# Gated linear attention and an MLP on one Trainium2 core: cumulative sums on two array tiles ahead of the scores, chunk 0 in halves of batches, statistics and gain on ScalarE, own buffers for the last chunk

## The chip, the cores and the metric

The kernel runs on one core of a Trainium2 chip. The metric is the device time of one execution in microseconds (us). Three runs of the kernel before took 469.5, 469.87 and 472.64 us; the median is 469.87 us.

## The reference

Four batches, eight heads, 768 positions, head size 48, all in fp32. A gated recurrence runs over the positions; its outputs, with the heads side by side (8 x 48 = 384 columns), are the rows `x` of a layer norm with gain, a two-layer MLP with 1536 hidden columns, and a residual sum:

```python
for t in range(S):
    state = alpha[:, :, t, :, None] * state + np.einsum('bhd,bhe->bhde', k[:, :, t], v[:, :, t])
    y[:, :, t] = np.einsum('bhd,bhde->bhe', q[:, :, t], state)
...
mu = np.mean(x, axis=-1, keepdims=True)
var = np.mean((x - mu) ** 2, axis=-1, keepdims=True)
xn = (x - mu) / np.sqrt(var + 1e-06) * g_ln
ch = np.maximum(xn @ w_ch1, 0.0) @ w_ch2
return (x + ch).astype(np.float32)
```

## The kernel before

**Chunks and batches.** The 768 positions are cut into six chunks `c` of 128, and there are four batches `b`. `attention(c, b)` (line 286) does one chunk of one batch; 24 of these generators exist, with the letters a to x (`a` is chunk 0, batch 0; `e` is chunk 1, batch 0). Chunk 0 is done as one block of 128 positions (`whole`); in the later chunks a block is two halves of 64 positions, which use TensorE as four tiles of 64 x 64.

**One attention.** ScalarE takes the logarithm of alpha into `la` (L299). TensorE sums it along the positions with a triangular matrix into `lps` (L304 for chunk 0, L312 later), and ScalarE makes the factors exp(+) and exp(-) of it (L317, L318). VectorE scales k and q (L320, L322), TensorE transposes them (`tps`, L347), ScalarE copies the transposes out (L352, L354, L357), TensorE makes the scores (`aps`, L364 or L369), VectorE masks them into `at` (L377, L380). TensorE makes the state's update (`ups`, L396), VectorE and GpSimd apply it (L411, L413), ScalarE copies the state into `va` (L403). TensorE makes the output (`yps`, L423), ScalarE copies it to `x` (L427), and `x` goes to DRAM (`kept`, L438) for the residual sum. Then comes the layer norm: VectorE's bn_stats and bn_aggr (L442, L443), ScalarE's Ln and Exp for 1/sqrt(var) (L446, L447), the normalised `xn` (chunk 0: VectorE, L451; later: a product of two columns on VectorE, L454, and ScalarE, L456), three transposes on TensorE (`xps`, L463) and one copy to `xT` on ScalarE (L465). The gain g_ln isn't applied here: it is multiplied into the rounded weights.

**Cumulative sums before.** In chunks 1 to 5 an even batch makes the sums of its own and of the next batch together (L307 to L312). The odd batch's alpha is loaded with its two halves of 64 positions exchanged (`load_exchanged`, line 118: two DMAs), so that the four products (two batches, two halves) lie on the four 64 x 64 tiles.

**Weights.** The MLP's weights come as 64-bit floats. `take_weights(i)` (letters A to L, line 235) loads one of 12 pieces and rounds it to fp32: four or more VectorE instructions (L217, L219, L221, L225, then L228 for w2; for w1 three instructions L232, which also multiply by the gain) and one ScalarE instruction (L223).

**The MLP.** Chunk 0 uses plain products: `hidden(c, j)` (L486) makes hidden columns j of all four batches, 512 columns wide, three products for each of twelve j; `project` (L498) makes the second layer. Chunks 1 to 5 use fast-multiplication schemes with fewer products: `hidden_product` (L733; 15 products in each of two rounds r, with recombination on VectorE, GpSimd and ScalarE, L741 to L776, and ReLUs L785) and `product` (L569; 20 products, L579 to L629). Their combined operands are made by `combine_first` (letter S, L685, on GpSimd: 17 sums over w1, partly in place), `combine_weights` (W, L529, VectorE), `combine_x` (X, L708) and `combine_hidden` (N, L556). The hidden activations of a chunk lie in one buffer `hT` (`bufs=1`), which every chunk uses in turn.

**What sets the order.** Each engine works through its queue in program order. The program order is written out by hand: `ORDER` (line 25) is a string of letters, and each letter lets one generator run to its next `yield`. M is the MLP of all chunks in a row, O loads residual rows, R are the ReLUs. A matmul in fp32 shows as two MATMUL records in the trace, a transpose as one.

Of the kernel before, what the change touches and what calls it, by code (L numbers as in the profile page):

```python
# [25 lines left out]
    "acaaabbadccdbabbaddcccaaaaacbbbaaaabbecccccbbbAadaccfafcbabdbbddefeAAddbafecccgA"  # L26
    "ddddhdbgagdhhCeffbaadhffffebbgaecefjCffiffeBadddfdccbeeccabgggddffccbdAdefffccji"
    "BjhjeeeBCBeDDCDjMMhheBMMkDEEGEeeOMMhMMMMegMMeCGFgGhFFhgGJMMMMihhhhhMMJiJlhhhhfMM"
    "MMEgHHgggegggFHHiiIgOMMMMegiIfeeeKggiKIILLKhlSSSSkkeLMMMWeeWWlgffhhhiikjMMkiiiii"
    "SSSSSfMhhMMOOhhhSgggjhjSSjMlWllffgijgMWfggXWXXmMXXXMMXXiOSMMMMMWOOiiSSijXiXXjjjj"  # L30
    "MMMMMMjkkSSnnkkiMMMMMMWMMjMjMMMMMjjkkMMMMRRjjjiiiRlkMMMkWMMmlnnkkkMMMllMMknkOMMR"
    "RMMMMMMMMllllmmMMMlmlMMMMMRMllllkkmRRRoMRMnjjikMMinnnnRiWWWMNMNNNjMMMnMnNNNmMMNN"
    "NlMppMMojkllkkMkkWMMMjjMRNNlNMMMMMmoooikMMMMMNNNkkMMllMMpMMlMMollmMMXnXnXmmXMXXX"
    "nnnXXMMMMnnMMmFmMmLXMMMMXpMMmmpqMMMMpprrnmMmmmKqpprprMMmnrrMMMMppppMMnpMqMMMMmmo"
    "ooMMMoMMMMOMMMMMpppMMMnnMOOOqJomRRRRMRRoooooMMRMroooMRMMMMMRMMRopqqmmCMpMMmotMNp"
    "ppNNnnRMoonMMNNNqqMMMnmnRMMMMMMMqmNNNNrNooMMqqqqqqNpMMMMopMpsrrMMNNMMqMMoMMoqsqq"
    "NNMsMMMMtttOMMprrqqssMsMppoXXXXXXDXXsssMXsXMMssrttXOOOrMMrMMMMrMMMrMtrrrtttMvMMM"
    "rrMMMMMMtssssuMMMMMMsssMtMMMMrrutttuuuqMMMMMMvRvqtvvMMMMMMRRMMuRRMMMMMRRqqquERMM"
    "vMvMMMttttvxsvRRrsMMsMMMMMMuRNNuuNMMMMMNNqRrNtuuuuMMrMMMuLuNqNNrqMMMMMtNNNNtrvvv"
    "vvvMMwMNvsssMMMMsttttsNwMOOxxMxuMMMNsxMMMtMMsMtuXXvvwwwuwXXXXXXMXwuMMMMMMMMMxxxv"  # L40
    "MMXXMMOMuuuMMMMMMMMMMMMMwxxvwMMMwMMvvMMuwwwwwMMMuMMMMMMMwwMMMMIMMMxxxRxxxRRRRMxM"
    "MMMRRRMMMMMRMORwwxxNNwwRMNNJMMMvvxNMMxNNuNuMMMMMMNNRMMMNMMMMMMMNNMGMMwwxwwMMxxxM"
    "NNMMMMMMNxxwvwMMvvXXMXXXXXOMMMMMMMXXMMMXMMMMMXMMMMMMMRMMMMMMMRRRMRMMMMMRMMAMMMMM"
    "MMKMMMMMMMROOOMMRMMMMMMMMMHRMMMMMRRNNNMMNMMMNNNNMMMMNRMMMMMNNMMMMNMMMNNNMMMMMMMM"
    "NBMMMMMM"
# [4 lines left out]
def kernel(  # L50
# [36 lines left out]
    nc = tc.nc  # L87
# [30 lines left out]
    def load_exchanged(to, src):  # L118

        for h in range(2):  # L120
            nc.sync.dma_start(to[halves[h]].rearrange("t i p d -> t (i p d)"),
                              src[halves[1 - h]].rearrange("t h d -> t (h d)"))

    def load(c, m, names):
# [3 lines left out]
        for n, src in (("a", alpha), ("k", k), ("q", q)):  # L128
            if n in names:
                t = raw.tile([P, 2, 2, NP, D], FP32, name=f"r{n}", tag=f"r{n}")  # L130
                step = 1 if n == "a" else 2
                for i in range(0, 2, step):
                    if n == "a" and c > 0 and i:
                        load_exchanged(t[:, 1], src[bs.start + 1, rows])
                        break
                    nc.sync.dma_start(
                        t[:, i:i + step].rearrange("t b i p d -> t b (i p d)"),
                        src[bs.start + i:bs.start + i + step, rows].rearrange("b t h d -> t b (h d)"))
                raws.update({(n, c, b): t[:, b - bs.start] for b in bs})
# [21 lines left out]
    def load_one(n):  # L161

        c, b = divmod(n, B)
        for n, src in (("a", alpha), ("k", k), ("q", q)):
# [4 lines left out]
            if n == "a" and b % 2:  # L169
                load_exchanged(t, rows)  # L170
            else:
                nc.sync.dma_start(t.rearrange("t i p d -> t (i p d)"),
                                  rows.rearrange("t h d -> t (h d)"))
# [8 lines left out]
    w1 = cpool.tile([P, NF, DF], FP32, name="w1")  # L182
    w2 = cpool.tile([P, NJ, DM], FP32, name="w2")
    small = cpool.tile([P, 2 * NF + 2], FP32, name="small")
    g_col, eps, least, g20 = small[:, :NF], small[:, NF:NF + 1], small[:, NF + 1:NF + 2], small[:, NF + 2:]
# [6 lines left out]
    for i in range(NJ // 2):  # L192
        cs, js = slice(2 * i * P, 2 * (i + 1) * P), slice(2 * i, 2 * (i + 1))
        pieces.append((w1[:, :, cs], w1_src[:, :, cs]))
# [12 lines left out]
    def round_weights(i):  # L207
# [19 lines left out]
        if i >= NJ // 2:  # L227
            stt(out=dst, in0=dst, scalar=2.0 ** -20, in1=hi.bitcast(FP32), op0=AOP.mult,  # L228
                op1=AOP.mult)
            return  # L230
        for f in range(NF):
            stt(out=dst[:, f], in0=dst[:, f], scalar=g20[:, f:f + 1], in1=hi[:, f].bitcast(FP32),  # L232
                op0=AOP.mult, op1=AOP.mult)
# [46 lines left out]
    nc.gpsimd.tensor_scalar_mul(g20, g_col, 2.0 ** -20)  # L280

    x_of, xT_of, hT_of, las, lpss = ({} for _ in range(5))
# [3 lines left out]
    def attention(c, b):  # L286
# [14 lines left out]
        yield  # L301
        if whole:
            lps = ps.tile([P, 512], FP32, name="lps", tag="a", bufs=3)
            nc.tensor.matmul(lps[:, :DM], tri, las.pop((c, b)), start=True, stop=True)  # L304
        elif b % 2 == 0:

            for d in range(2):  # L307
                to = lpss[c, b + d] = ps.tile([P, 512], FP32, name="lps", tag="a", bufs=3)
                a = las.pop((c, b + d))
                for s in range(2):  # L310
                    h = halves[s ^ d]
                    nc.tensor.matmul(to[halves[s], :DM], tri[h, h], a[h], start=True, stop=True)  # L312
        yield
        if not whole:
            lps = lpss.pop((c, b))
# [111 lines left out]
        nc.scalar.copy(out=x, in_=yps.rearrange("t a b d -> t (a b d)"))  # L427
# [12 lines left out]
        stats = work.tile([P, 6], FP32, name="stats", tag="stats")  # L440
        mv = work.tile([P, 2], FP32, name="mv", tag="mv")
        nc.vector.bn_stats(stats, x)  # L442
        nc.vector.bn_aggr(mv, stats)  # L443
        yield
        rstd = work.tile([P, 2], FP32, name="rstd", tag="rstd")
        nc.scalar.activation(out=rstd[:, :1], in_=mv[:, 1:2], func=AFT.Ln, bias=eps)  # L446
        nc.scalar.activation(out=rstd[:, :1], in_=rstd[:, :1], func=AFT.Exp, scale=-0.5)  # L447
        yield
        xn = work.tile([P, DM], FP32, name="xn", tag="xn", bufs=2)
        if whole:  # L450
            nc.vector.tensor_scalar(out=xn, in0=x, scalar1=mv[:, 0:1], scalar2=rstd[:, :1],  # L451
                                    op0=AOP.subtract, op1=AOP.mult)
        else:
            nc.vector.scalar_tensor_tensor(out=rstd[:, 1:], in0=mv[:, 0:1], scalar=-1.0,  # L454
                                           in1=rstd[:, :1], op0=AOP.mult, op1=AOP.mult)
            nc.scalar.activation(out=xn, in_=x, func=AFT.Identity, scale=rstd[:, :1],  # L456
                                 bias=rstd[:, 1:])
# [7 lines left out]
        nc.scalar.copy(out=xT_of[c][:, :, b], in_=xps)  # L465
# [15 lines left out]
    def hidden(c, j):  # L481
        if j == 0:
            hT_of[c] = work.tile([P, NJ, B, P], FP32, name="hT", tag="hT", bufs=1)
        hps = ps.tile([P, B, P], FP32, name="hps", tag="m", bufs=3)
# [357 lines left out]
```

## Time and profile before

| | |
|---|---|
| median of 3 runs | 469.87 us (469.5 to 472.64) |
| the profiled execution itself | 469.91 us |
| its span in the profile | 468.1 us, so 1.8 us lie around the span |
| TensorE (PE) busy | 445.0 us |
| VectorE (DVE) busy | 357.8 us |
| ScalarE (ACT) busy | 214.4 us |
| GpSimd (POOL) busy | 175.4 us |
| mean granted TensorE clock | 0.995 |

In the profile's rows a group is named by line, engine, operation and tile ("L312 PE MATMUL lps<-la,consts"). PEld is TensorE's loading of weights, SPq the queue of DMA issues on SyncE. A time in the timeline counts from the start of the span; the bracket at a row's end is the engine's idle time ahead of it, with what ended it. A matmul's recorded duration overlaps with that of the next one, so the rate of TensorE is read from the distance between starts.

### The profile page before, as it was taken

To read this page: it belongs to the slowest core of one execution; us is meant where nothing else is said; L and a number is where in the kernel's file an instruction comes from. 1 tells how busy PE (TensorE), PEld (TensorE's weight loads), DVE (VectorE), ACT (ScalarE), POOL (GpSimd) and SP (SyncE) were. 2 spreads that over 40 slices of the span, in tenths; PEclk is the share of its full clock that TensorE was granted. 3 is DMA by queue.
4 is the path that set the end of the run, shared out by engine and by line. 5 is a ranking of instruction groups with operands and counts; after the bars stand their busy time and mean duration, and the time that the engine had idled before them with its cause. 6 is when DMAs were issued, how large, how long until landed. Compare 5 with 4: busy or idle time off the path is not lost.

```text
span 468.1 us, 10317 instructions
## 1 busy us (share of the span) xinstructions
PE 445.0 (95%) x4050; PEld 369.2 (79%) x4050; DVE 357.8 (76%) x704; ACT 214.4 (46%) x467; POOL 175.4 (37%) x201
## 2 busy tenths in 40 slices
PE   5978999999999999999999999999999999898996
PEld 4856445656678898988889988899998899887896
DVE  3798998998697888785687685867875787765683
ACT  5377474553435555334664444666333451413200
POOL 1010001167576620436440526550326531444513
PEclk9998999999999999999999999999999999999999
DMA  8978967514312340334530226230132000220001
GB/s 274 253 211 225 279 200 200 159 42 142 115 43 61 77 129 18 87 86 101 139 103 1 68 71 170 88 84 3 56 114 38 1 1 0 95 75 1 1 17 52
DMA packets 58232, 45.42 MB, mean 97 GB/s; under 512 B 26908, under 2 KB 54300, under 8 KB 58184
## 3 DMA queue, kind: packets, MB, share of 16 engines
q1 hardware_dynamic: 57640, 44.63, 34.1%
q8 instruction: 32, 0.52, 0.5%
q10 hardware_dynamic: 544, 0.13, 0.2%
q14 instruction: 16, 0.13, 0.1%
HBM read 35.22 MB, written 9.53 MB: 96 GB/s over the span
## 4 chain that ended last, share of the span: by engine, by line
PE 62%; DVE 22%; POOL 6%; ACT 4%; issue 3%; DMA 2%; SPq 0%; POOLq 0%; DVEq 0%; ACTq 0%
PE ops L569 23%; PE hps L733 20%; PE aps L369 4%; PE hps L486 3%; PE yps L423 3%; PE tps L347 2%; DVE at L380 2%; PE ups L396 2%; DMA ws<-in_moe_w_ch_dram 2%; PE ops L498 2%; DVE ws L225 2%; DVE w L219 1%; DVE ws L529 1%; PE xps L463 1%; DVE sum L556 1%
## 5 line engine op out<-in xcount | busy, mean ns | idle before, releaser
L585 POOL TENSOR_TENSOR ob<-ob,u 128x192 f32<-128x192 f32 x40 | 27.8, 704 | 100.0 <-DVE ob L582 76.0
L733 PE MATMUL hps<-sum,w 128*128 128x256 f32 x240 | 60.8, 385 | 1.9 <-DVE hT L776 1.1
L413 POOL TENSOR_TENSOR st<-st,gate 112x192 f32<-112x192 f32 x36 | 20.7, 576 | 86.8 <-DVE st L411 62.4
L733 PEld LDWEIGHTS hps<-sum,w 128*128 128x128 f32 x240 | 44.1, 190 | 9.4 <-DVE hT L776 1.8
L569 PE MATMUL ops<-w,hT 128*128 128x192 f32 x280 | 50.4, 329 | 0.0
L785 ACT ACTIVATE hT<-hT 128x512 f32<-128x512 f32 x60 | 35.0, 622 | 26.1 <-POOL hT L755 14.3
L569 PEld LDWEIGHTS ops<-w,hT 128*128 128x128 f32 x280 | 45.6, 190 | 1.4 <-DVE sum L556 0.6
L403 ACT COPY va<-st 64x192 f32<-64x192 f32 x80 | 27.8, 347 | 25.1 <-POOL st L413 24.3
L486 PE MATMUL hps<-xT,w 128*128 128x512 f32 x72 | 32.3, 598 | 0.8 <-ACT hT L489 0.8
L498 PE MATMUL ops<-w,hT 128*128 128x384 f32 x96 | 32.4, 489 | 0.0
L733 PE MATMUL hps<-xT,w 128*128 128x256 f32 x120 | 31.5, 385 | 0.8 <-DVE hT L765 0.7
L380 DVE COPY_PREDICATED at<-consts,aps 64x512 f32<-64x512 int32 x40 | 29.2, 731 | 3.3 <-PE aps L369 2.3
L569 PE MATMUL ops<-ws,sum 128*128 128x192 f32 x160 | 29.3, 329 | 0.8 <-DVE u L579 0.8
L569 PE MATMUL ops<-ws,hT 128*128 128x192 f32 x160 | 29.6, 328 | 0.1
L357 ACT COPY at<-tps 64x512 f32<-64x512 f32 (+1 forms) x40 | 23.2, 579 | 11.6 <-PE tps L347 6.9
L369 PEld LDWEIGHTS aps<-at,kT 48*64 48x64 f32 x640 | 22.0, 138 | 8.1 <-issue 5.0
L752 POOL TENSOR_TENSOR hT<-hT,u 128x512 f32<-128x512 f32 x10 | 12.8, 1285 | 40.8 <-DVE u L751 40.7
L579 DVE TENSOR_TENSOR ob<-ops,ob 128x192 f32<-128x192 f32 x50 | 17.5, 352 | 13.5 <-POOL ob L585 4.2
L347 PE MATMUL tps<-consts,qk 128*112 128x128 f32 x176 | 25.7, 278 | 2.2 <-DVE qk L322 1.2
L423 PEld LDWEIGHTS yps<-va,at 128*64 128x64 f32 (+1 forms) x768 | 24.1, 137 | 4.4 <-issue 2.8
L498 PEld LDWEIGHTS ops<-w,hT 128*128 128x128 f32 x96 | 17.7, 190 | 12.2 <-DVE w L228 1.0
L569 PEld LDWEIGHTS ops<-ws,sum 128*128 128x128 f32 x160 | 26.0, 190 | 1.4 <-DVE u L579 1.0
(155 smaller groups left out, 1021.1 us busy)
## 6 DMA issues: line engine op xcount, KB each, us to landing
ws<-in_moe_w_ch_dram SPq DMA_DIRECT2D x12, 768.0 KB, 4.8
kept<-x SPq DMA_DIRECT2D x24, 192.0 KB, 2.4
ob<-kept SPq DMA_DIRECT2D x24, 192.0 KB, 2.9
va<-in_v_dram SPq DMA_DIRECT2D x40, 96.0 KB, 3.4
out_dram<-ob SPq DMA_DIRECT2D x19, 192.0 KB, 1.9
ra<-in_alpha_dram SPq DMA_DIRECT2D x14, 192.0 KB, 4.1
rk<-in_k_dram SPq DMA_DIRECT2D x6, 384.0 KB, 4.0
rq<-in_q_dram SPq DMA_DIRECT2D x6, 384.0 KB, 4.3
```

The source lines that it names most:

```text
L347: nc.tensor.transpose(tps[:, p], qk_of(c, b)[:, i, p].rearrange("p a b -> p (a b)")[:, :R], ident)
L357: nc.scalar.copy(out=at[rows[j], :, j], in_=tv[rows[j]])
L369: nc.tensor.matmul(aps[i][halves[1 - i], p, s], kT[rs, p, s], at[rs, p, i, s], start=True, stop=True)
L380: nc.vector.copy_predicated(out=at[h, :, i], data=aps[i][h], mask=mask[h, h].unsqueeze(1).unsqueeze(1).broadcast_to([HS, NP, 2, HS]))
L403: nc.scalar.copy(out=to[h, s, i], in_=st[h])
L423: nc.tensor.matmul(yps[halves[s], i, p], at[rs, p, i, s], va[rs, 0 if whole else s, i, p], start=True, stop=True)
L486: nc.tensor.matmul(hps, w1[:, f, j * P:(j + 1) * P], xT_of[c][:, f], start=(f == 0), stop=(f == NF - 1))
L498: nc.tensor.matmul(ops_of[b], hT_of[c][:, j, b], w2[:, j], start=(j == 0), stop=(j == NJ - 1))
L569: nc.tensor.matmul(acc, lhs[:, j], rhs[:, j], start=(j == 0), stop=(j == NT - 1))
L585: getattr(nc.gpsimd, f"tensor_{op}")(x, x, y)
L733: nc.tensor.matmul(acc[:, i], w, b, start=True, stop=True)
L785: nc.scalar.activation(out=x, in_=x, func=AFT.Relu)
```

## The change

Seven things change together:

1. **Cumulative sums.** Each batch makes its own sums, on the two tiles (0,0) and (1,1) of the array (each half of the positions to the same half of the output). No alpha is loaded exchanged any more, and an alpha load is one DMA for two batches (in chunk 0 still one for each). In the new program 16 of the 20 sums of chunks 1 to 5 stand directly ahead of another batch's scores `aps`, which use the tiles (0,1) and (1,0); the other four, all of chunk 1, stand in the first part of the program, ahead of `yps`, `ups`, chunk-0 `aps` and `tps`.
2. **Chunk 0 in halves.** `hidden(h, j)` makes the columns of two batches (256 wide instead of 512), so there are 72 products instead of 36, each half as wide; letters Y, Z are the two halves of the first layer, P, Q those of the second. In TensorE's order the first `hps` of chunk 0 now stands after only two of the four `xps` of chunk 0.
3. **Statistics on ScalarE.** The copy to `x` also gives the row sum, a Square with the negative mean as bias gives the row's squared deviations; bn_stats, bn_aggr and the product of two columns leave VectorE.
4. **The gain on ScalarE.** The copy of `xps` to `xT` becomes three ScalarE multiplications by a column of g. The rounding of w1 then ends with one VectorE instruction over 768 columns instead of three over 256.
5. **combine_first on VectorE.** The 17 sums over w1 leave GpSimd, and w1 is laid out by piece.
6. **The last chunk in own buffers.** The hidden activations of chunk 5 lie in `at`, `qk` and `va` buffers, which attention no longer needs then; its sums of x and its scratch lie in other such buffers. The first-layer products of chunk 5 have a letter of their own (V), and `ORDER` mixes them with the second-layer products of chunk 4.
7. **ORDER** is written anew throughout.

The core of the diff:

```diff
-        elif b % 2 == 0:
-            for d in range(2):
-                to = lpss[c, b + d] = ps.tile([P, 512], FP32, name="lps", tag="a", bufs=3)
-                a = las.pop((c, b + d))
-                for s in range(2):
-                    h = halves[s ^ d]
-                    nc.tensor.matmul(to[halves[s], :DM], tri[h, h], a[h], start=True, stop=True)
+        else:
+            for h in halves:
+                nc.tensor.matmul(lps[h, :DM], tri[h, h], a[h], start=True, stop=True)
...
-        nc.scalar.copy(out=x, in_=yps.rearrange("t a b d -> t (a b d)"))
+        act(out=x, in_=yps.rearrange("t a b d -> t (a b d)"), func=AFT.Copy, accum_out=mean)
...
-        nc.vector.bn_stats(stats, x)
-        nc.vector.bn_aggr(mv, stats)
+        nc.scalar.mul(mean, mean, -1.0 / DM)
+        act(out=xn, in_=x, func=AFT.Square, bias=mean, accum_out=dev)
...
-            nc.vector.scalar_tensor_tensor(out=rstd[:, 1:], in0=mv[:, 0:1], scalar=-1.0,
-                                           in1=rstd[:, :1], op0=AOP.mult, op1=AOP.mult)
+            nc.scalar.mul(off, mean, rstd)
...
-        nc.scalar.copy(out=xT_of[c][:, :, b], in_=xps)
+        for f in range(NF):
+            nc.scalar.mul(xT_of[c][:, f, b], xps[:, f], g_col[:, f:f + 1])
...
-        for f in range(NF):
-            stt(out=dst[:, f], in0=dst[:, f], scalar=g20[:, f:f + 1], in1=hi[:, f].bitcast(FP32),
-                op0=AOP.mult, op1=AOP.mult)
+        stt(out=dst, in0=dst, scalar=2.0 ** -20, in1=hi.bitcast(FP32), op0=AOP.mult, op1=AOP.mult)
...
-    def hidden(c, j):
-        hps = ps.tile([P, B, P], FP32, name="hps", tag="m", bufs=3)
+    def hidden(h, j):
+        bs = slice(2 * h, 2 * h + 2)
+        hps = ps.tile([P, 2, P], FP32, name="hps", tag="m", bufs=3)
         for f in range(NF):
-            nc.tensor.matmul(hps, w1[:, f, j * P:(j + 1) * P], xT_of[c][:, f],
+            nc.tensor.matmul(hps, w1[:, j // 2, f, j % 2 * P:][:, :P], xT_of[0][:, f, bs],
...
-        add, sub = nc.gpsimd.tensor_add, nc.gpsimd.tensor_sub
+        add, sub = nc.vector.tensor_add, nc.vector.tensor_sub
...
+    def third_of(c, t, h):
+        if c + 1 == NCB:
+            return late_of["h"][t * 2 + h]
+        return hT_of[c][:, t * NT:(t + 1) * NT, h * HB:(h + 1) * HB]
...
+    def buffers_of_last():
+        va = [raw.tile([P, 2, 2, 2, NP, D], FP32, name="va", tag="va").rearrange(
+            "t b s i p d -> t (b s i p d)") for _ in range(2)]
+        h = [t.rearrange("k p i s t -> k (p i s t)") for t in ats]
+        h += [t.rearrange("t n p i c -> t (n p i c)") for t in qks[:3]]
+        h.append(va[0][:, :NT * HB * P])
...
     def mlp():
+        for c in range(1, NCB):
+            if c + 1 < NCB:
+                yield from hidden_products(c)
             for n in SECOND:
                 yield from product(c, n)
...
-    turns |= {"M": mlp(), "S": combine_first(), "W": combine_weights(), "R": relus(),
+    turns |= {"M": mlp(), "V": hidden_products(NCB - 1), "S": combine_first(), "W": combine_weights(), "R": relus(),
```

## The prediction

> **What bounds the kernel now.** I read the windows by stage first, then TensorE's timeline inside each stage, then the groups for prices. The rows of the windows give start and end, length, then busy time and instructions of PE, PEld, DVE, ACT, POOL, and last granted clock, DMA share and GB/s. The cuts lie at the first `hps` of chunk 0 (46.87), the end of its first layer (80.9), the start of chunk 1's MLP (125.9), the start of chunk 5's MLP (407.4), its second layer (437.5) and the last matmul (464.3).
>
> ```profile
> 0.00:46.87 46.87, 36.29 (x530) 28.66 (x530) 34.52 (x72) 28.56 (x66) 5.17 (x11) 0.96 0.84 241
> 46.87:80.90 34.03, 33.21 (x179) 16.00 (x178) 32.01 (x53) 19.18 (x34) 2.27 (x4) 1.00 0.75 224
> 80.90:125.90 45.00, 43.31 (x330) 27.21 (x331) 39.34 (x72) 21.75 (x47) 22.84 (x29) 1.00 0.38 113
> 125.90:407.40 281.50, 278.71 (x2738) 249.17 (x2737) 214.19 (x436) 133.34 (x299) 120.57 (x133) 1.00 0.26 69
> 407.40:437.50 30.10, 26.89 (x121) 22.42 (x120) 19.12 (x34) 8.63 (x15) 15.81 (x14) 1.00 0.13 39
> 437.50:464.30 26.80, 26.56 (x161) 25.76 (x160) 18.25 (x41) 2.95 (x7) 7.82 (x11) 1.00 0.05 16
> 464.30:468.10 3.80, 0.02 (x1) 0.00 (x0) 0.36 (x1) 0.00 (x0) 0.90 (x2) 0.84 0.30 104
> ```
>
> From 46.87 on TensorE has hardly any gaps; VectorE, the next, has 94% in the second row, 87% in the third, 76% in the fourth. So after 46.87 the time is the length of TensorE's queue, and ahead of it TensorE idles 10.6 us while it waits for others. The other hole is in chunk 5's first layer, which has only itself to run:
>
> ```profile
> 49.99 10.47 PE L486 MATMUL hps<-xT,w 128*128 128x512 f32 x24
> 60.39 1.14 PE L423 MATMUL yps<-va,at 128*64 128x48 f32 x32
> ...
> 177.03 0.88 PE L312 MATMUL lps<-la,consts 64*64 64x384 f32 x8
> 177.84 1.57 PE L569 MATMUL ops<-more,sum 128*128 128x192 f32 x8
> ...
> 409.74 1.13 PE L733 MATMUL hps<-sum,ra 128*128 128x256 f32 x4 [1.36 <-DVE sum L708]
> 410.71 1.03 PE L733 MATMUL hps<-sum,w 128*128 128x256 f32 x4
> 411.57 1.03 PE L733 MATMUL hps<-xT,rk 128*128 128x256 f32 x4
> ...
> 425.60 1.13 PE L733 MATMUL hps<-sum,w 128*128 128x256 f32 x4 [1.10 <-DVE hT L776]
> ```
>
> Prices by distance of starts: 24 matmuls of 512 columns in 60.39 - 49.99 = 10.40 us, 0.433 each; four of 256 columns in 0.86 us, 0.215 each; the cumulative sums of two batches 177.84 - 177.03 = 0.81 us.
>
> A rule to weigh here: the Trainium skill, "Perfetto Trace Analysis", Identifying the Most-Contended Engine, says that matmul busy time misleads and that headroom is judged by MFU and the weight loads' busy share. The page has PEld at 79%, which by that rule would leave 0.21 x 468 = 98 us in TensorE's queue, and a matmul removed would then buy nothing where something else paces. The starts decide: the matmuls of 256 columns follow each other at 0.215 us while one load takes 0.190, so loads are 88% busy in a stretch that has no gap at all. I take the queue as the bound, with about 3 us of stalls in 46.87 to 407.
>
> **The change, part by part.** *Cumulative sums.* Before: ten pairs at 0.81 = 8.1 us. Each batch alone uses two tiles, two passes each, still 0.81 us (the passes of a tile follow each other): 20 x 0.81 = 16.2 us if nothing runs beside. In the program's order 16 of the 20 stand directly ahead of scores on the other two tiles, and TensorE does run ahead on a free tile past an instruction that waits for its own:
>
> ```profile
> 363.08 1.02 PE L369 MATMUL aps<-at,kT 48*64 48x64 f32 x27
> 363.89 0.25 PE L396 MATMUL ups<-rv,qk 64*64 64x48 f32 x1
> 363.95 0.22 PE L369 MATMUL aps<-at,kT 48*64 48x64 f32 x2
> 363.99 0.22 PE L396 MATMUL ups<-rv,qk 64*64 64x48 f32 x1
> ```
>
> All `aps` stand ahead of all `ups` in the program, yet they alternate here. Scores take about 0.95 us (363.08 to the last at 364.06), more than 0.81, so 16 sums should vanish under them. Left are the four early ones, 3.2 us. That is -4.9 us, and five pairs that stood between full-array products no longer break that mode: I give this another -0.7 us, between 0 and -1.0 (0.2 us at most for each). A rule speaks against it: the Trainium skill, "TensorEngine Tiling (Array Packing)", Gotcha 1: PSUM Pressure, says that different row tiles cannot access one PSUM bank at the same time, and both halves of a batch's `lps` now lie in one tile of 512 columns. By the rule a sum takes 1.6 us, 0.65 us sticks out of the scores, and 16 x 0.65 + 4 x 1.6 = 17 us replaces 8.1: +9 us. But the pairs of before also put two row tiles into each `lps`, and the four still took 0.81 us. I take the row.
>
> *Halves in chunk 0.* 144 matmuls at 0.215 = 31.0 us against 72 at 0.433 = 31.2: nothing, on the path. Each needs `xT` of two batches. Ahead of the first `hps` TensorE's queue now lacks a batch's `tps` (0.44 us), one `aps` with `ups` (1.44), one `yps` (1.07) and two `xps` (0.66), and has 0.8 more of sums: 2.8 us of work moves behind it. VectorE's queue there loses four batches' bn_stats and aggregates (4 x 0.73 us), two `xn` (1.0), and parts of roundings and masks that ORDER puts later; by program order and the rows' means it holds some 9 us less. So the first `hps` could come 0 to 9 us sooner; I take 6, as ACT and the loads (DMA 84% of the stretch) do not get shorter. Gain: 6 - 2.8 = 3.2 us, rounded to -3, between +3 and -6.
>
> *Statistics and gain.* VectorE loses per run 13.2 (L442) + 4.4 (L443) + 5.4 (L454) + 0.6 (L682), and 7.7 - 5.8 = 1.9 at the roundings (L232 against six of 0.96, L228's undisturbed price): 25.5 us. It hardly waits on the path after 80 us, so this is worth nothing there by itself; its use is room for combine_first. ScalarE gains: 24 small products at 0.20 (L447) 4.9; 24 Squares, whose price lies between 0.49 (L318, no column) and 0.71 (L456, two columns), 0.65 with its sum, 15.6; 20 products of columns at 0.29 (L446) 5.8; 72 scaled copies of 128 columns at 0.40 (L446 plus 127 columns at 0.85 ns, from L427 and L741) 28.8, less the 11.4 of L465; the row sum in L427, 0 to 0.2 each, 2.4; halved ReLUs +2. Together +48, to 262 us or 57% of the span. In the first 126 us, where eight batches fall, it is +17 on 69.5: 69% of the stretch. That is cover enough on average; behind each late ACT instruction stand the copies of `tps` and the ReLUs that free the `hps` banks, for which PE waits. I charge +2 us for new waits, between 0 and +8.
>
> *combine_first.* 15 sums of 512 columns at 0.69 (L556) and four of 256 at 0.46: 12.2 us more on VectorE against 26.8 less on GpSimd (L685). It overwrites w1 in place, so its later sums wait until chunk 0's last `hps` has read w1, and what VectorE holds behind them waits too; but by program order VectorE is then some 10 us ahead of TensorE. W's sums, 1.48 us where both engines work on SBUF and 0.94 elsewhere, get shorter by up to 4 us. Net on the path 0.
>
> *Loads.* Four alpha loads of two batches lose two DMA issues each (1.2 us of SPq for the two), six single ones lose one. The order of the rest stays; hidden behind SP's other issues: 0 to -1, inside the early term.
>
> *Last chunk.* 120 matmuls at 0.215 = 25.9 us took 437.53 - 407.36 = 30.2: 4.3 us of stalls, in the timeline as waits for L708, L765, L776, where VectorE and GpSimd trail. Mixed with chunk 4's second layer (160 matmuls) each has other work to stand on: -4, between 0 and -4.5. The end stays: 3.8 us after the last matmul.
>
> **Sum.** -4.9 - 0.7 + 0 - 3 + 2 - 4 = -10.6 us. From the profiled execution, 469.9 us (468.1 of span and 1.8 around it; the median of the runs is the same 469.87), this gives 459.3, so 459 us.
>
> **The rivals.** *A, the early gain or the last chunk's fails:* the first `hps` comes no sooner, since loads hold it (3 + 2.8 us back: 465), or GpSimd's chain at the end still sets the pace (4 back: 463), or both (469); mid 466. For it: DMA at 84%. Against: DVE's 34.5 us of 46.87 with the statistics in the middle of it. *B, the sums do not hide:* either the order between tiles or the bank rule holds; 16 x 0.81 = 13 us come back: 472 us, no change. For it: no row shows sums and scores together. Against: the alternating rows above. *C, slower: ScalarE becomes what TensorE waits for.* Each attention adds 48 / 24 = 2.0 us of serial ScalarE work; if 0.6 us of each turns into a PE wait, 24 x 0.6 = 14 us cancel the gain plus the margin, and a full 1.2 us gives 459 + 29 - 2 = 486. For it: the statistics, the gain, copies and ReLUs all queue on one engine in the first 126 us. Against: at 69% there, and of PE's waits on ACT the profile has under 5 us in all. *D, the change doesn't shorten TensorE's queue* is B.
>
> **How the numbers follow.** The likeliest case, all steps within their bounds: 0.69, own range 452 to 465, prediction 459. A: 0.13. B: 0.07. C: 0.11. The range leaves out about 0.07 below 452 (the stalls of the middle vanish as well) and 0.12 above 470: 452 to 470. A per cent, 4.7 us, is about what a measurement of this kernel can tell from no change. Faster by over 1% (under 465.2): the first case and a third of A, 0.73. Within 1%: the rest of A and most of B, 0.15. Slower (over 474.6): C and a little of B, 0.12.
>
> **What would show it.** `lps` rows whose starts lie among `aps` rows with no gap behind them: right; the full-array product after them 1.7 us or more after the first `lps`: B. First `hps` of chunk 0 at about 41 us: right; at 46 or later: A. Chunk 5's first-layer products without bracketed waits over 0.5 us: right. VectorE's busy time about 345 us, ScalarE's about 262, GpSimd's about 147. If PE's waits for ACT sum to over 10 us, C; the prediction is wrong above all if TensorE's gaps after the first `hps` grow.

## The result, and the profile after

The changed kernel takes 458.52 us (median of four runs, 458.32 to 459.46); the kernel before took 470.29 us (median of four, 469.5 to 472.64) beside it. The ratio is 0.9746 with a 95% interval of 0.9707 to 0.9784: faster by 2.5%. The prediction was 459.0. The profiled execution took 459.46 us with a span of 457.7 us, 1.8 us around it as before.

The busy times of the changed kernel, from its page, and then its windows, cut at the first `hps` of chunk 0 (38.23), inside the stage up to chunk 1's MLP, at the start of chunk 5's MLP (380.15) and at 420.1. The columns are those of the windows before: start and end, length, PE, PEld, DVE, ACT, POOL, granted clock, DMA share, GB/s.

```profile
PE 441.1 (96%) x4122; PEld 381.0 (83%) x4122; DVE 338.5 (74%) x626; ACT 249.8 (55%) x643; POOL 152.3 (33%) x164
```

```profile
0.00:38.23 38.23, 31.46 (x417) 23.96 (x418) 27.24 (x57) 25.19 (x63) 4.30 (x9) 1.00 0.86 259
38.23:60.00 21.77, 21.00 (x304) 17.54 (x302) 18.32 (x29) 19.59 (x52) 2.57 (x5) 1.00 0.86 256
...
80.00:100.00 20.00, 18.81 (x171) 14.60 (x170) 17.56 (x28) 14.78 (x40) 4.17 (x4) 1.00 0.63 189
100.00:127.00 27.00, 25.89 (x214) 16.46 (x213) 24.89 (x39) 11.00 (x26) 2.52 (x2) 1.00 0.28 75
127.00:380.00 253.00, 250.90 (x2356) 223.46 (x2354) 186.24 (x352) 149.32 (x390) 103.83 (x108) 1.00 0.27 73
380.00:420.10 40.10, 40.05 (x206) 36.19 (x206) 30.39 (x60) 8.24 (x16) 19.48 (x17) 1.00 0.07 21
```

Three things are to be seen. Ahead of the first `hps` TensorE idles 38.23 - 31.46 = 6.8 us, where it idled 10.6 before. In the stretch from 380 to 420, where most of chunk 5's first layer now lies, it idles 0.05 us; in the stretch of that layer in the kernel before it idled 3.2. And from 38 to 127 TensorE still has small holes (3.9 us in 88.8, the row not shown among them), with ScalarE at 90% in the second row and VectorE at 92% in the fourth.

The sums and the scores, in TensorE's timeline (start, duration, then line, tile and shape; the `ups` in the last row is the next step):

```profile
65.03 0.54 PE L289 MATMUL lps<-la,consts 64*64 64x384 f32 x2
65.20 0.40 PE L344 MATMUL aps<-at,kT 48*64 48x64 f32 x6
65.40 0.49 PE L289 MATMUL lps<-la,consts 64*64 64x384 f32 x2
65.42 0.80 PE L344 MATMUL aps<-at,kT 48*64 48x64 f32 x21
66.01 0.25 PE L371 MATMUL ups<-rv,more 64*64 64x48 f32 x1
```

The 32 scores begin 0.17 us after the sums and run between and beside their four passes; sums and scores together take 66.01 - 65.03 = 0.98 us. Scores alone took 0.81 up to the next `ups` in the kernel before, sums alone 0.81.

**Where the time came from.** In either trace I add up the distances from each matmul's start to the next one's, by line. From the first matmul's start to the last one's it is 461.2 us before and 450.8 after, 10.4 less. The MLP products of chunks 1 to 5 (`hps` and `ops`) account for 274.8 before and 265.6 after: -9.1. Sums and scores of chunks 1 to 5 account for 29.2 and 27.1: -2.1. All the rest, the early stage above all, comes out 0.8 longer. Of the 9.1 us, 4.0 are the stalls of chunk 5's first layer (4.25 beyond 0.216 us for each product before, 0.26 after). The other 5.1 lie in the middle (125.9 to 407.3 us before, 138.6 to 380 after): 76 places before, 44 after, at which the step from a full-array product to the next matmul lasted 0.02 to 0.3 us longer than the usual 0.216 (`hps`) or 0.163 us (`ops`), mostly by 0.09 or 0.10 (7.7 against 4.7 us in sum), and the longer stalls there (2.7 against 0.7 us).

The granted clock differs too. In the windows of the kernel before, cut at the clock's own steps, TensorE is busy 1.50 of 3.41 us, and in the next 3.42 us it runs at half clock:

```profile
36.78:40.19 3.41, 1.50 (x24) 0.89 (x16) 3.30 (x8) 3.33 (x9) 0.00 (x0) 1.00 1.10 322
40.19:43.61 3.42, 3.39 (x39) 3.30 (x40) 2.47 (x6) 2.44 (x8) 1.05 (x2) 0.50 0.88 210
```

3.4 us at half clock cost up to 1.7 us. The changed kernel has no such step before its last matmul.

### The profile page after: what moved, and what is told of

The parts are those of the page before. It is cut to its first block, busy times and chain, and to the rows that moved or that the text cites. A ratio compares the mean times of both kernels' runs of the same rounds, so it can differ in the third digit from the quotient of the medians.

```text
span 457.7 us, 10476 instructions
## 1 busy us (share of the span) xinstructions
PE 441.1 (96%) x4122; PEld 381.0 (83%) x4122; DVE 338.5 (74%) x626; ACT 249.8 (55%) x643; POOL 152.3 (33%) x164
## 4 chain that ended last, share of the span: by engine, by line
PE 64%; DVE 14%; ACT 10%; POOL 5%; DMA 3%; issue 3%; POOLq 0%; SPq 0%; DVEq 0%; ACTq 0%
PE ops L573 24%; PE hps L750 23%; PE ops L474 4%; DMA gate<-row 3%; PE tps L322 3%; PE aps L344 2%; PE yps L398 2%; POOL ob L589 2%; DVE ws L213 2%; DVE w L207 2%; PE ups L371 1%; PE xps L436 1%; DVE w L215 1%; DVE sum L724 1%; ACT at L332 1%
## 5 line engine op out<-in xcount | busy, mean ns | idle before, releaser
L750 PE MATMUL hps<-sum,w 128*128 128x256 f32 x192 | 47.8, 381 | 0.1
L750 PEld LDWEIGHTS hps<-sum,w 128*128 128x128 f32 x192 | 35.4, 190 | 5.7 <-ACT hT L758 0.9
L573 PE MATMUL ops<-w,hT 128*128 128x192 f32 x224 | 39.8, 327 | 0.0
L573 PEld LDWEIGHTS ops<-w,hT 128*128 128x128 f32 x224 | 36.5, 190 | 0.7 <-DVE ob L583 0.2
L462 PE MATMUL hps<-xT,w 128*128 128x256 f32 x144 | 34.2, 383 | 0.5 <-ACT hT L465 0.5
L583 DVE TENSOR_TENSOR ob<-ops,ob 128x192 f32<-128x192 f32 x50 | 17.4, 352 | 20.6 <-POOL ob L589 10.8
L750 PE MATMUL hps<-xT,w 128*128 128x256 f32 x120 | 31.2, 383 | 0.2 <-DVE hT L782 0.2
L439 ACT ACTIVATE xT<-xps,small 128x128 f32<-128x128 f32 x72 | 20.9, 366 | 18.7 <-PE xps L436 18.6
L462 PEld LDWEIGHTS hps<-xT,w 128*128 128x128 f32 x144 | 26.1, 190 | 4.3 <-ACT hT L465 0.9
L801 ACT ACTIVATE hT<-hT 128x512 f32<-128x512 f32 x48 | 27.6, 623 | 3.4 <-DVE hT L782 1.6
L474 PEld LDWEIGHTS ops<-w,hT 128*128 128x128 f32 x96 | 17.8, 190 | 12.6 <-DVE w L215 1.4
L398 PE MATMUL yps<-va,at 128*64 128x48 f32 (+1 forms) x768 | 26.9, 224 | 1.4 <-ACT xT L439 0.7
L322 PEld LDWEIGHTS tps<-consts,qk 128*112 128x112 f32 x176 | 19.3, 134 | 7.2 <-ACT at L332 1.9
```

The lines of the kernel that those rows point to most:

```text
L322: nc.tensor.transpose(tps[:, p], qk_of(c, b)[:, i, p].rearrange("p a b -> p (a b)")[:, :R], ident)
L398: nc.tensor.matmul(yps[halves[s], i, p], at[rs, p, i, s], va[rs, 0 if whole else s, i, p], start=True, stop=True)
L439: nc.scalar.mul(xT_of[c][:, f, b], xps[:, f], g_col[:, f:f + 1])
L462: nc.tensor.matmul(hps, w1[:, j // 2, f, j % 2 * P:][:, :P], xT_of[0][:, f, bs], start=(f == 0), stop=(f == NF - 1))
L474: nc.tensor.matmul(ops_of[b], hT_of[c][:, j, b], w2[:, j], start=(j == 0), stop=(j == NJ - 1))
L573: nc.tensor.matmul(acc, lhs[:, j], rhs[:, j], start=(j == 0), stop=(j == NT - 1))
```

## The experiments

The theory after reading the two traces: the gain is the sums under the scores, the mixed last chunk and fewer breaks, and the moves between VectorE, ScalarE and GpSimd are worth nothing by themselves. The rival: these moves, with the order laid out for them, are what carries the gain. "More than the changed kernel" is the distance between medians, to 458.52 us, taken on another chip (the kernel before has medians of 469.83 to 470.43 us on the five chips used, so 0.6 us can't be told from nothing); a distance to the kernel before is taken from its runs on the same chip.

**Sums on the whole array.** One product with a block-diagonal 128 x 128 triangle takes the place of the two on two tiles:

```diff
-            for h in halves:
-                nc.tensor.matmul(lps[h, :DM], tri[h, h], a[h], start=True, stop=True)
+            nc.tensor.matmul(lps[:, :DM], both, a, start=True, stop=True)
```

> The changed kernel (458.5 us) with the cumulative sums of chunks 1 to 5 made by one product with a block-diagonal triangle on the whole array, in the same places. Such a product costs 2 x 0.323 = 0.65 us and can't run beside the scores. If the sums vanish under the scores and TensorE's queue is the bound, 16 of them come out of their cover and break the full-array mode, 16 x (0.65 + 0 to 0.2), and the four early ones change by -0.16 each: +10 to +13 us, 468 to 472 us. If the sums were not hidden in the changed kernel, or were not on the path: within 2 us of 458.5.

Measured: 464.48 us (ratio 0.9879, 0.9835 to 0.9923), 6.0 more than the changed kernel: about half of what hiding was to be worth. Its timeline at the same place of the program as above:

```profile
63.94 0.81 PE L289 MATMUL lps<-la,consts 128*128 128x384 f32 x2
64.68 1.02 PE L344 MATMUL aps<-at,kT 48*64 48x64 f32 x27
65.49 0.25 PE L371 MATMUL ups<-rv,more 64*64 64x48 f32 x1
```

Nothing overlaps now: 0.74 for the sum, 0.81 for the scores, 1.55 against 0.98. So the hiding is shown. In the later chunks a pair took 0.91 to 0.94 up to `ups`, so a hidden sum stuck out 0.10 to 0.13 there, and nothing where a full-array product follows (1.15 against 1.13). What was off is where it counts: chunk 1's MLP began at 138.26 us here and at 138.61 in the changed kernel. Six of the sixteen hidden sums lie ahead of that point. From the first `hps` (37.22 here, 38.23 there) to it, this kernel takes 101.05 us against 100.39: six uncovered sums, 3.4 us at 0.57 each, cost 0.7, so the early stage isn't set by the length of TensorE's queue. The ten behind it make the loss: 5.0 us between the two traces from there to the last matmul, where ten at 0.63 would be 6.3.

**Own sums alone, in the old order.** In the kernel before, each batch makes its own sums at its own place, without the exchanged loads:

```diff
-        if whole:
-            lps = ps.tile([P, 512], FP32, name="lps", tag="a", bufs=3)
...
+        lps = ps.tile([P, 512], FP32, name="lps", tag="a", bufs=3)
+        a = las.pop((c, b))
...
+            for h in halves:
+                nc.tensor.matmul(lps[h, :DM], tri[h, h], a[h], start=True, stop=True)
```

> The kernel before (470.3 us) with each batch making its own sums on two tiles and no exchanged load, but in the old order, in which they don't stand ahead of scores. If the gain lies in the place beside the scores: 20 x 0.81 instead of 10 x 0.81, +8 us, and up to 2 us more for mode changes, so 477 to 480 us. If the gain lay in the simpler loads and the shorter wait for a partner batch: 466 to 470 us.

Measured: 479.01 us (ratio 1.0187, 1.0137 to 1.0236), as expected: 8.8 us slower than the kernel before. The sums are a gain only at the places that the new order gives them. Here the half clock lasted 6.8 us instead of 3.4, which is part of it.

**The last chunk in turn.** The end of ORDER is rewritten, so that chunk 4's second layer ends before chunk 5's first begins; the buffers stay as changed:

```diff
-    "XXXMMVVRNXXXXMMMXNXMVVVNVVVVVVXNMMMNVVXMNMMVVVRVVVVVVMNMVVVVVVVVAMMMNVVNRRMMMRRR"
...
+    "XXXMMRNXXXXMMMXNXMNXNMMMNXMNMMMNMAMMMNNMMMMMNNMMNOMMMMMMMOMMMOOLVVVVVVVVVVVVVVVV"
...
```

> The changed kernel with the rest of chunk 4's second layer first and chunk 5's first layer after it, in turn, own buffers kept. If the mixing is what removed the stalls of chunk 5's first layer: +4 us, 462 to 463 us, with waits of TensorE for VectorE's results between the products. If the own buffers or a lighter VectorE did it: 458 to 459.5 us.

Measured: 462.08 us (ratio 0.983, 0.9787 to 0.9873), as expected: the mixing is worth 3.6 us. The own buffers weren't undone by themselves.

**Statistics back on VectorE.** bn_stats, bn_aggr and the product of two columns return to VectorE, at the steps where they stood:

```diff
-        nc.scalar.mul(mean, mean, -1.0 / DM)
-        act(out=xn, in_=x, func=AFT.Square, bias=mean, accum_out=dev)
+        nc.vector.bn_stats(stats, x)
+        nc.vector.bn_aggr(mv, stats)
...
-            nc.scalar.mul(off, mean, rstd)
+            nc.vector.scalar_tensor_tensor(out=off, in0=mv[:, 0:1], scalar=-1.0, in1=rstd,
+                                           op0=AOP.mult, op1=AOP.mult)
```

> The changed kernel with bn_stats, bn_aggr and the product of two columns back on VectorE (+23 us of VectorE, -25 of ScalarE). If TensorE's queue is the bound and the early gain comes from the order of chunk 0: 457.5 to 460.5 us, the first product of chunk 0 within 2 us of 38.2. If the early gain comes from a VectorE freed of the statistics: that product 3 to 6 us later, 462 to 465 us.

Measured: 484.12 us (ratio 1.0321, 1.0255 to 1.0387), 25.6 more than the changed kernel. Both expectations missed, and by the largest step of the study. Chunk 1's MLP began at 137.46, even 1.15 us earlier; all of the loss came later. One place, in the timelines of ScalarE, VectorE and TensorE of this kernel in turn (the bracket is the idle time ahead, and what ended it):

```profile
338.28 0.29 ACT L424 ACTIVATE few<-mv,small 128x1 f32<-128x1 f32 x1 [6.63 <-DVE mv L422]
...
341.44 1.16 ACT L332 COPY at<-tps 64x512 f32<-64x512 f32 x2
342.62 0.59 ACT L327 COPY kT<-tps 112x512 f32<-112x512 f32 x1
...
346.83 1.30 ACT L433 ACTIVATE xn<-x,few 128x384 f32<-128x384 f32 x2 [3.02 <-DVE few L431]
```

```profile
344.44 1.46 DVE L355 COPY_PREDICATED at<-consts,aps 64x512 f32<-64x512 int32 x2 [2.02 <-PE aps L344]
...
346.65 0.21 DVE L431 SCALAR_TENSOR_TENSOR few<-mv,few 128x1 f32<-128x1 f32 x2
```

```profile
343.26 1.02 PE L344 MATMUL aps<-at,kT 48*64 48x64 f32 x27 [1.51 <-ACT kT L327]
...
348.19 0.90 PE L439 MATMUL xps<-consts,xn 128*128 128x128 f32 x3 [3.43 <-ACT xn L433]
348.88 2.77 PE L576 MATMUL ops<-ws,sum 128*128 128x192 f32 x8
```

Read it from the top. ScalarE stands 6.63 us at Ln, for which VectorE's `mv` is late. Behind Ln in its queue are the copies of the transposes, so `kT` is late, and TensorE waits 1.51 us for its scores. VectorE waits 2.02 us for these scores with its mask, and behind the mask in its queue stands the product of two columns, for which ScalarE waits with `xn` 3.02 us, and TensorE with `xps` 3.43 us. The last row is the price on top: eight products take 2.77 us where they take 1.46 otherwise, at half clock (347.08 to 353.9); TensorE had stood still for 2.32 of the 3.41 us from 343.67 to 347.08. In this trace half clock lasts 13.7 us before the last matmul, in the changed kernel none.

**VectorE's load without the chain.** The changed kernel, with bn_stats and bn_aggr issued as well, for nobody:

```diff
         act(out=xn, in_=x, func=AFT.Square, bias=mean, accum_out=dev)
+        nc.vector.bn_stats(stats, x)
+        nc.vector.bn_aggr(mv, stats)
```

> The changed kernel, with bn_stats and bn_aggr of x issued on VectorE as well, at the place where the kernel before had them, and their results read by nobody: VectorE gets 24 x 0.73 = 17.5 us of work back and waits for x as before, but the chain x, Square, Ln, Exp, xn stays on ScalarE. Theory H (what cost e3_stats_on_vector its 25.6 us is the chain's two handovers between ScalarE and VectorE, inside the distance that the order leaves between x and xps): 458 to 463 us. Rival L (VectorE's load itself is what TensorE ends up waiting for, through late roundings, masks and sums): 470 us or more, most of the 25.6.

Measured: 463.69 us (ratio 0.9866, 0.9847 to 0.9886), 5.2 more than the changed kernel, and just past the upper end of what theory H gave it. The load alone is some 5 of the 25.6 us; it comes little by little (chunk 2's MLP is 1.9 us later, chunk 3's 3.3, chunk 4's 4.5). The other 20 are not VectorE's load: they come with the handovers and with the half clock that goes with these waits (13.7 us of it, which cost up to 6.9), and these two weren't measured apart. Nor is the early stage bound by the amount of VectorE's work: 6.6 us of these instructions stand ahead of chunk 1's MLP, which begins only 0.75 us later (139.36).

**Statistics on VectorE, but earlier.** bn_stats, bn_aggr and the negated mean stand two steps of the order earlier, and Ln, Exp, the product of two columns and `xn` are all on ScalarE:

```diff
             carry(0, raws["v", c + 1, b][1])
+        nc.vector.bn_stats(stats, x)
+        nc.vector.bn_aggr(mv, stats)
+        nc.vector.tensor_scalar_mul(mean, mv[:, 0:1], -1.0)
```

> The changed kernel with bn_stats and bn_aggr on VectorE as in e3_stats_on_vector, but issued two steps of the order earlier (with the carry of the state, when x has long been copied), with the mean negated there too, so that from Ln to xn the chain runs on ScalarE alone: VectorE has some 22 us more than in the changed kernel and ScalarE some 29 us less, but neither engine waits for the other between x and xps. Theory H (the handovers inside the short distance cost e3_stats_on_vector its 25.6 us, and VectorE's load costs the 5.2 us of e8_stats_beside): 461 to 466 us. Rival (statistics on VectorE are dear in this order wherever they stand): 470 us or more.

Measured: 469.29 us over ten runs (466.5 to 470.97; ratio 0.9987, 0.9963 to 1.001), 10.8 more than the changed kernel: outside both expectations. Taking away one handover and giving the other more room returns 15 of the 25.6 us. The remaining one is still there in the waits of this kernel (engine, tile and line; the releaser; us in total, times, longest):

```profile
ACT few L425 <- DVE mv L417: 18.9, 9, 5.3
```

In the kernel with both handovers the like wait was 36.5 us in 14 places, and a second one, for the product of columns, 26.5 us in 16. Half clock lasted 10.2 us in this trace. The two of the ten runs at a mean clock of 1.0 took 466.5 and 467.06 us, so the half clock is about 2.5 us of the median. With 5.2 for the load some 3 us are left for the remaining handover; this division is worked out, not measured apart.

**Statistics on ScalarE alone, in the old order.** The same move as in the change, made in the kernel before:

```diff
-        nc.scalar.copy(out=x, in_=yps.rearrange("t a b d -> t (a b d)"))
+        act(out=x, in_=yps.rearrange("t a b d -> t (a b d)"), func=AFT.Copy, accum_out=mean)
...
-        nc.vector.bn_stats(stats, x)
-        nc.vector.bn_aggr(mv, stats)
...
+        act(out=xn, in_=x, func=AFT.Square, bias=mean, accum_out=dev)
```

> The kernel before, in its old order, with only the statistics moved to ScalarE (row sum in the copy to x, Square with its sum, no bn_stats, no bn_aggr); the gain stays in the weights. Theory (worth nothing on the path by itself, as the prediction's step said; the order of before leaves room for the chain on either engine): 468 to 472 us. Rival 1 (VectorE's 17.5 us less is a gain of its own in any order): 460 to 466. Rival 2 (ScalarE's 17 us more in the first 126 us delays TensorE): 474 or more.

Measured: 473.47 us (ratio 1.0068, 1.0046 to 1.009), between the theory and rival 2: 3.6 us slower than the kernel before on that chip (469.83). The first `hps` came at 50.72 instead of 46.87, and chunks 1 to 5 begin 2.2 to 4.3 us later than there; half clock lasted 6.8 us instead of 3.4. So the move is a small loss in the old order, and it is what the new order needs.

**Statistics split by chunk.** VectorE for chunks 0 and 1, ScalarE for the rest:

```diff
+        early = c < 2
...
-            nc.scalar.mul(off, mean, rstd)
+            if early:
+                nc.vector.scalar_tensor_tensor(out=off, in0=mv[:, 0:1], scalar=-1.0, in1=rstd,
+                                               op0=AOP.mult, op1=AOP.mult)
+            else:
+                nc.scalar.mul(off, mean, rstd)
```

> The changed kernel with the statistics of chunks 0 and 1 on VectorE as in e3_stats_on_vector, and of all later chunks on ScalarE. In e3_stats_on_vector chunk 1's MLP began at 137.46 us against 138.61 in the changed kernel; all of its loss came later. Theory (up to there ScalarE is as short as VectorE, and the 1.15 us stay a gain): 457 to 458.3 us, the fastest of all. Rival (the 1.15 us were work left for later, or the handovers cost as much here): 458.5 to 461.

Measured: 459.07 us (ratio 0.9756, 0.9733 to 0.9779), in the rival's range and no faster than the changed kernel. The 1.15 us didn't return: chunk 1's MLP began at 138.81, and the first `hps` came at 40.35 instead of 38.23, with 6.8 us of half clock ahead of and around it. The one run at a mean clock of 1.0 took 458.51 us, so without half clock there is no gain either.

**The gain in the weights.** The gain goes back into w1, and `xT` is one copy again:

```diff
-        for f in range(NF):
-            nc.scalar.mul(xT_of[c][:, f, b], xps[:, f], g_col[:, f:f + 1])
+        nc.scalar.copy(out=xT_of[c][:, :, b], in_=xps)
```

> The changed kernel with g multiplied into w1 when the weights are unpacked, as before, so that xT is one copy of three slices instead of three scaled copies: ScalarE loses 24 x 2 instructions, about 9.5 us of busy time, VectorE splits 6 unpackings in three. Theory (three overlapped copies lie beside other work; ScalarE is nowhere the bound after 60 us): 457 to 459.5 us. Rival (ScalarE at 90% from 38 to 60 us holds TensorE in that stage, and the stage sets the end): 456 or less.

Measured: 459.2 us (ratio 0.9771, 0.9753 to 0.9788), which can't be told from the changed kernel: where the gain is applied is worth nothing here.

**combine_first back on GpSimd.**

```diff
-        add, sub = nc.vector.tensor_add, nc.vector.tensor_sub
+        add, sub = nc.gpsimd.tensor_add, nc.gpsimd.tensor_sub
```

> The changed kernel with combine_first's 19 additions back on GpSimd, at the same places of the order and without the one-element memsets that kept the two engines in step before. Theory (the move is net 0 on the path, as the prediction's step said): 458 to 460.5 us. Rival (GpSimd's 1.41 us per addition against VectorE's 0.69 makes the last sums of w1 late for chunk 1's first products): 463 or more, with PE waits on POOL at the start of chunk 1's first layer.

Measured: 464.49 us (ratio 0.9879, 0.9855 to 0.9902), 6.0 more than the changed kernel: the rival's time, though not by its mechanism. No late sum of w1 is waited for. VectorE, which has 19 additions less to do, is busy *longer*, 345.9 us against 338.5. Its timeline at one place, then GpSimd's in the same kernel:

```profile
86.58 0.96 DVE L215 SCALAR_TENSOR_TENSOR w<-w,ws 128x768 f32<-128x768 f32 x1
...
88.71 4.96 DVE L215 SCALAR_TENSOR_TENSOR w<-w,ws 128x768 f32<-128x768 f32 x1
93.59 0.34 DVE L386 TENSOR_TENSOR st<-ups,st 112x192 f32<-112x192 f32 x1
```

```profile
89.00 1.26 POOL L699 TENSOR_TENSOR rk<-ra,w 128x512 f32<-128x512 f32 x1
90.22 0.72 POOL L699 TENSOR_TENSOR ra<-ra,w 128x256 f32<-128x256 f32 x1
90.91 0.72 POOL L699 TENSOR_TENSOR rk<-ra,w 128x256 f32<-128x256 f32 x1
91.59 1.26 POOL L699 TENSOR_TENSOR rq<-w 128x512 f32<-128x512 f32 x1
```

One rounding step of 0.96 us takes 4.96 while four additions run on GpSimd, and 0.96 + 1.26 + 0.72 + 0.72 + 1.26 = 4.92: it stood still for all four. The Trainium skill says just that ("SBUF — State Buffer", Who interferes with whom): a VectorE instruction with two inputs in SBUF contends with a GpSimd instruction that reads SBUF, and the loser blocks instead of sharing. Behind it the state's update `st` starts at 93.59; in the changed kernel it starts at 90.86, and there that rounding step took 1.15. TensorE's `yps` then waits 2.19 us for this update; ahead of the same two `yps` in the changed kernel TensorE waits 0.66, and for ScalarE. In all, the five lines of the rounding (L205 to L215) take 58.9 us here and 48.7 in the changed kernel. The two of them with one input got longer too (L205 0.55 to 0.64, L209 0.56 to 0.72 us on average), so two inputs are not the whole of it. Chunk 1's MLP begins at 143.65 us instead of 138.61: 5.0 us, nearly all of the loss, arise in the stage ahead of it.

**combine_first on VectorE alone, in the old order.**

```diff
-        add, sub = nc.gpsimd.tensor_add, nc.gpsimd.tensor_sub
+        add, sub = nc.vector.tensor_add, nc.vector.tensor_sub
...
-            nc.vector.memset(tok[:, m:m + 1], 0.0)
-            nc.gpsimd.memset(tok[:, m:m + 1], 0.0)
```

> The kernel before with combine_first's 19 additions on VectorE at the places that the old order gave them, without the one-element memsets. Theory K (in e5_first_on_gpsimd VectorE's own sums and roundings ran up to five times as long while GpSimd added beside them, 10 us in all, so taking the additions off GpSimd is a gain in either order): 464 to 467.5 us. Rival 1 (net 0, the prediction's step): 468.5 to 471. Rival 2 (places made for GpSimd put 12 us of VectorE's queue in front of what TensorE waits for): 472 or more.

Measured: 472.14 us (ratio 1.0042, 1.0019 to 1.0064): no gain, a loss of 1.7 us. Chunk 1's MLP began at 129.74 instead of 125.92, and half of that came back later. This trace has a second stretch of half clock (3.4 us, 6.8 in all instead of 3.4), which can be up to 1.7 us of it. Theory K, that the contention makes the move a gain in either order, fell.

**Chunk 0's products whole.** The products of the second half's places are made 512 columns wide, the first half's letters (Y) are taken out of ORDER, and the second layer's letters that stood ahead of the last Z stand behind it:

```diff
-        bs = slice(2 * h, 2 * h + 2)
-        hps = ps.tile([P, 2, P], FP32, name="hps", tag="m", bufs=3)
+        bs = slice(0, B)
+        hps = ps.tile([P, B, P], FP32, name="hps", tag="m", bufs=3)
```

> The changed kernel with chunk 0's first products for all four batches at once (512 columns, as before), issued at the places of the second half's products; the second products that stood ahead of the last of them stand right behind it. The same columns run, so TensorE's work is equal; what goes is the first half's 15.5 us of products that fill TensorE while batches 2 and 3 are still on their way. Theory (the halves are worth the earlier start, the prediction's -3, as other work to stand on in the stage to 138 us): 460 to 464 us. Rival 1 (that stage is paced by VectorE's and ScalarE's chains, and the fill is worth nothing): 457.5 to 459.5. Rival 2 (the fill is worth most of its length): 465 or more.

Measured: 481.48 us (ratio 1.0231, 1.0205 to 1.0256), 23 more than the changed kernel: rival 2, and beyond the 15.5 us that were the length of the fill. Its windows of the stage that lost, with the columns as above:

```profile
80.00:100.00 20.00, 15.34 (x141) 8.47 (x135) 17.81 (x29) 14.80 (x39) 4.32 (x4) 1.00 0.63 188
100.00:127.00 27.00, 15.80 (x163) 10.54 (x164) 24.77 (x38) 14.53 (x35) 2.53 (x2) 0.62 0.37 89
```

TensorE stands still for 11.2 of 27 us, at a mean clock of 0.62 (27.3 us of this trace lie at half clock), while VectorE is 92% busy, as in the changed kernel. There the same stretch has 1.1 us of holes. Chunk 1's MLP begins at 158.67 us instead of 138.61, 20.1 later. Up to there TensorE is idle for 26.0 us instead of 10.6, which is 15.4, just the length of the fill, and busy for 132.7 us instead of 128.0 with the same columns: 4.7 us that go with the half clock. So chunk 0's products are what TensorE does while other engines' chains set the pace. Which chain that is isn't shown: VectorE is the busiest, but 6.6 us more of its work moved the end of the stage by 0.75 us above. The edit also moved twelve steps of the second layer, so it measures the cover of both layers together, not the halves by themselves; that wasn't tried apart.

## Why the prediction was right, and where not

The time was right to 0.5 us, and the sum, -10.6, meets the 10.4 us found between the starts. But several of its terms were wrong and cancel; that the sum came out so near is luck in part. The starts give -2.1 for the sums, -5.1 for breaks and stalls of the middle, -4.0 for the last chunk and +0.8 for the rest, where the prediction had -4.9, -0.7, -4 and -1.

- **The bound.** Right after about 138 us, where ten sums on the whole array turned into 6 us. Wrong ahead of it: I took the queue as the bound "from 46.87 on". In the changed kernel TensorE's queue doesn't set the pace up to 138 us: six sums out of their cover cost 0.7 us there, not 3.4, and taking away work that TensorE does meanwhile cost 20. Which of the other engines' chains sets it stays open.
- **Cumulative sums, -4.9.** The mechanism is right: tiles run past a waiting instruction of other tiles, and the sums vanish under the scores. The bank rule that was weighed against it would have cost +9; both halves of a batch still write one `lps`, and no sum stood out by the 0.65 us that it gives. The size was too large: the account by starts gives -2.1. The four early sums take 3.3 us against 3.2 predicted, but the sixteen hidden ones stick out 0.1 us each in most places, which I had put at nothing: I had taken the scores at 0.95 us, and up to the next `ups` they take 0.81. That is some 1.6 of the missing 2.8 us. The account also holds TensorE's waits that fall among sums and scores, 2.3 us after (at 76 and 110 us) and 1.2 before (at 30 us).
- **Breaks between full-array products, -0.7.** Mis-sized the other way. I counted five pairs of sums. The new order breaks the runs of full-array products less often: 76 breaks became 44, worth 3.0 us, and the long stalls of the middle fell by 2.0. This term and the "net 0" of the stalls should have been -5.
- **Halves of batches, -3 with the early start.** The first `hps` came at 38.23, even earlier than the 41 I gave it, and idle time ahead of it fell by 3.8 us. But the account by starts shows no net gain outside the MLP of chunks 1 to 5 and the sums (+0.8, with up to 1.7 us of half clock gone). The early start was spent again in the stage up to 138 us, whose new waits I charged at +2. That I called the halves "nothing, on the path" was the wrong view: they are the cover of chunk 1's attention.
- **Statistics to ScalarE, "worth nothing there by itself".** This step failed. In the old order it is a loss of 3.6 us, which is near. In the new order it is what holds the time: 25.6 us are lost without it, of which VectorE's load is 5.2. I priced instructions on VectorE's queue; what the traces show in their place is a chain that waits in two queues (36.5 us at Ln, 26.5 at `xn`), in an order that leaves little time between `x` and `xps`. ScalarE's work was sized at +48 us; the rows add up to that nearly, but they overlap (a Square with its read of the sum: 0.61 us from start to next start, against 0.62 + 0.19), and busy time rose by 35.4, to 249.8. PE's waits on ACT sum to 5.2 us, so rival C is ruled out.
- **combine_first, "net on the path 0".** This failed too: 6.0 us in the new order, with VectorE's instructions stretched beside GpSimd's additions; 1.7 us lost by the move in the old. I had seen W's sums stretched from 0.94 to 1.48 us beside GpSimd and had counted only their time, not what is queued behind.
- **Last chunk, -4.** Right: 3.6 by undoing it, 4.0 by its stalls.
- **Loads, 0 to -1.** Not tried by itself.

The singles don't add up. Each of three parts alone in the old order costs (+8.8, +3.6, +1.7); undoing the sums, the last chunk, combine_first or the statistics in the new order costs 6.0, 3.6, 6.0 and 25.6. Their sum, 41 us, is far over the 11.8 gained: ORDER was laid out for all of them at once, and with any part undone it is an order made for another kernel. So these numbers say what each part carries in this order; they don't say what share of the gain is its own. How much of it the order would bring without any of the parts stays open. No run beat the changed kernel.

## What to carry to other kernels

Price a moved instruction by the queues that its chain has to stand in, not by its duration alone: a two-column product of 0.2 us behind a mask can stop three engines. Read, stage by stage, whether TensorE's queue or another engine's chain sets the pace; in the second kind of stage shortening TensorE's queue is worth little (0.7 of 3.4 us here), and having TensorE's own independent work there is worth up to its length (15.4 us of idle time here). A hand-written order and the engine assignment are one thing: test a part in the order that it is meant for.

## What the runs showed of the hardware

- **Half clock after half-idle windows.** In the 14 traces the granted clock changes only at steps of 3.41 us. There are 13 drops from full clock; in the 3.41 us ahead of them no matmul ran for 1.50 to 2.98 us. Every such window with 2.0 us or more of idle time led to a drop, none with less than 1.50 did, and between these both occurred. The idle time need not be in one piece. Half clock then lasted 3.4 or 6.8 us, in one case 20.5 us with the idle time going on.
- **Tiles run past each other.** Scores on two tiles start 0.17 us after sums on the other two that stand ahead of them in the program; the pair takes 0.98 us against 0.81 for either alone. So on TensorE the program order doesn't hold across tiles.
- **A sum output on ScalarE is an instruction of its own**, ACTIVATION_READ_ACCUMULATOR, 0.19 to 0.20 us, which overlaps with its neighbours to about 0.1 us.
- **VectorE beside GpSimd.** One instruction with two SBUF inputs was lengthened by the full duration of the four GpSimd additions that ran in that time (0.96 to 4.96 us).
